# Loading the first batch's v in pieces of 120 and 8 partitions behind a one-partition transfer

## The chip, the core and the metric

The kernel runs on one core of a Trainium2 chip. The metric is the device time of one execution in microseconds (us); less is better. Before the change the median of three runs is 319.89 us (319.6 to 319.95).

## What is computed

Attention with keys and values projected along the sequence (eight batches, eight heads, 1024 positions, head size 64, 64 projected positions), then a layer in which two products of the same input compete and the larger one passes on. All inputs and outputs are float32.

```python
k_proj = einsum('ks,bhsd->bhkd', E, k);  v_proj = einsum('ks,bhsd->bhkd', F, v)
scores = q @ k_proj^T / sqrt(64)
attn   = exp(scores - max) / sum(exp(scores - max))
x      = (attn @ v_proj) laid out as 8192 tokens x 512
out    = maximum(x @ w1, x @ w2) @ w_out          # 512 -> 1024 -> 512
```

## The kernel before

Everything is computed in 16 bits from inputs that are converted as they are loaded. q, k and v of a batch each lie in one tile of 128 partitions (`k_sb`, `q_sb`, `v_sb`): partition p holds positions 8p to 8p + 7 of every head. `load` (line 107) issues such a transfer, or that of some heads only, from GpSimd (POOL in the profile), which also does all the conversions' transfers. The order of all work on all engines is the order of the program's text, written out by hand; a framework adds the semaphores. It also keeps a limited set of semaphores for the transfers that GpSimd issues, so that a transfer can wait in GpSimd's queue until an earlier one has landed.

At the start SyncE loads E, F and the first two heads of k. GpSimd then loads for batch 0: k of heads 2 and 3, q of heads 0 to 3, k and q of heads 4 to 7 (lines 116 to 118), then v in four loads of two heads each:

```python
    for h in range(0, H, 2):
        load(tiles[0], "v", v, 0, h, h + 2)          # lines 122, 123
```

Behind them stand fourteen pieces of the weights w1 and w2 (lines 128 to 142; four at line 130, ten at line 139), the output weights `wo_sb` (line 143), and the loads of batch 1 (line 108, and line 1019 for q). GpSimd issues them one after another.

Batch 0's own steps are written out from line 959 on. `step_eft` turns E and F, `step_kv` (line 183; its matmuls are at line 195, its copies at 205 and 207) projects k or v, `step_qt` turns q (311, 316), `step_sc` forms scores (340) and their exponentials (380), `step_dn` the sums over them (352, 388), `step_inv` the reciprocals (427), `step_at` the products with v (352, 443). `warm` (153) are matmuls on a constant. The order around v is

```python
    step_sc(t, 1, 0)
    step_kv(t, 0, 2, "v"); step_kv(t, 2, 4, "v")
    step_dn(t, 1, 0); step_sc(t, 1, 1); step_at(t, 0, 0); step_at(t, 0, 1); step_inv(t, 1, 0)
    step_kv(t, 4, 8, "v", True, copy=nc.scalar.copy, between=lambda: step_dn(t, 1, 1))
```

(lines 984 to 992, joined here). So the projection of v takes the first two loads one after the other, later the third, and then, behind another sum, the fourth.

Then comes the layer. maximum(a, b) is computed as b + relu(a - b): `wd_sb` = w1 - w2 is formed by VectorE (DVE, lines 541 and 549) as the pieces of weights land, TensorE multiplies x by it (line 525), and turns w2 (557) for a small product w2 x w_out (634). From unit 1 on both large products use a scheme of seven block products with sums of blocks (lines 746 and 838); `T_sb` holds four sums of blocks of `wo_sb` and of that small product, and is written by VectorE at line 597. It is declared at line 580.

Of the kernel before, what the change touches and what calls it, by code (L numbers as in the profile page):

```python
# [10 lines left out]
FP16 = mybir.dt.float16  # L11
# [8 lines left out]
def kernel(  # L20
# [12 lines left out]
    nc = tc.nc  # L33
# [3 lines left out]
    DM = moe_w1.shape[0]  # L37
    DF = moe_w1.shape[1]
    NC = S // 128
# [11 lines left out]
    const = ctx.enter_context(tc.tile_pool(name="const", bufs=1))  # L51
# [13 lines left out]
    def mm_bank(dtype=FP32, n=None):  # L65
        if n is None:
            n = turn.pop(0)
            turn.append(n)
        return ps.tile([128, 512 if dtype == FP32 else 1024], dtype, tag=f"mm{n}", name="mm_ps")
# [37 lines left out]
    def load(t, n, src, b, h0, h1):  # L107
        nc.gpsimd.dma_start(
            out=t[n][:, h0:h1],
            in_=src[b, h0:h1].rearrange("h (p c) d -> p h c d", c=NC),  # L110
        )

    tiles = {b: {} for b in range(B)}
    for n in ("k", "q", "v"):
        alloc(tiles[0], n)
    for h0 in (0, H // 2):
        for n, src in (("k", k), ("q", q)):
            load(tiles[0], n, src, 0, h0 + 2 * ((h0, n) == (0, "k")), h0 + H // 2)
            if (h0, n) == (0, "k"):
                ident = const.tile([128, 128], FP32)  # L120
                make_identity(nc, ident)
    for h in range(0, H, 2):
        load(tiles[0], "v", v, 0, h, h + 2)

    w1_sb = big(1).rearrange("p (r f) -> p r f", r=NDC)
    w2_sb = big(2).rearrange("p (r f) -> p r f", r=NDC)
# [1 line left out]
    for g in range(2):  # L128
        for w_sb, w in ((w2_sb, moe_w2), (w1_sb, moe_w1)):
            nc.gpsimd.dma_start(  # L130
                out=w_sb.rearrange("p (g z) f -> p g z f", z=2)[:, g, :, 0:256],
                in_=w.rearrange("(g p z) f -> p g z f", p=128, z=2)[:, g, :, 0:256],
            )
    for w_sb, w, f0, f1 in (
        (w2_sb, moe_w2, 256, 512), (w1_sb, moe_w1, 256, 512), (w2_sb, moe_w2, 512, DF),
        (w1_sb, moe_w1, 512, 768), (w1_sb, moe_w1, 768, DF),
    ):
        for z in range(2):
            nc.gpsimd.dma_start(
                out=w_sb.rearrange("p (g z) f -> p g z f", z=2)[:, :, z, f0:f1],  # L140
                in_=w.rearrange("(g p z) f -> p g z f", p=128, z=2)[:, :, z, f0:f1],
            )
    nc.gpsimd.dma_start(out=wo_sb, in_=moe_w_out.rearrange("(r p) f -> p r f", p=128))

    ones16 = const.tile([128, 512], FP16)
# [427 lines left out]
    NG = NFB // 2  # L573
    NX = NDC // 2
    CH = DM // 2
# [1 line left out]
    last = len(units) - 1  # L577
    U = {(b, o): {"n": n, "b": b, "o": o, "t": tiles[b]} for n, (b, o) in enumerate(units)}

    T_sb = const.tile([128, 4, NG + NX, CH], FP16)  # L580


    box = {}
# [536 lines left out]
    for b in range(3, B):  # L1120
        t = tiles[b]
        n = 2 * b - 3
# [13 lines left out]
    for i, (new, old) in enumerate(zip([*groups[1:], none], groups)):  # L1136
        n, h = divmod(i + 2, 2)
# [54 lines left out]
    for reg in regs:  # L1192
# [4 lines left out]
        out=mm_bank()[0:1, 0:1], lhsT=ones16[:, 0:1], rhs=ones16[:, 0:1], start=True, stop=True  # L1197
# [166 lines left out]
```

## Time and profile before

| | us |
|---|---|
| median of 3 runs | 319.89 |
| profiled execution, its own time | 320.29 |
| its span, first to last instruction | 318.5 |
| TensorE (PE) busy | 311.8 |
| VectorE (DVE) busy | 241.1 |
| ScalarE (ACT) busy | 206.0 |
| GpSimd (POOL) busy | 41.4 |

Times in the profile are microseconds from the span's start. PE is TensorE's matmuls, PEld its weight loads, which overlap them. A row of a timeline has the start, the length, the engine and line, the operation, what it writes and reads, and a count; a bracket at its end says how long the engine had been idle and what it waited for. A wait for several things is put down to the one that came last. In rows of transfers the size is that of the destination, in 16 bits.

### The profile page before, as it was taken

To read this page: it belongs to the slowest core of one execution; us is meant where nothing else is said; L and a number is where in the kernel's file an instruction comes from. 1 tells how busy PE (TensorE), PEld (TensorE's weight loads), DVE (VectorE), ACT (ScalarE), POOL (GpSimd) and SP (SyncE) were. 2 spreads that over 40 slices of the span, in tenths; PEclk is the share of its full clock that TensorE was granted. 3 is DMA by queue.
4 is the path that set the end of the run, shared out by engine and by line. 5 is a ranking of instruction groups with operands and counts; after the bars stand their busy time and mean duration, and the time that the engine had idled before them with its cause. 6 is when DMAs were issued, how large, how long until landed. Compare 5 with 4: busy or idle time off the path is not lost.

```text
span 318.5 us, 9309 instructions
## 1 busy us (share of the span) xinstructions
PE 311.8 (98%) x3922; PEld 253.8 (80%) x3922; DVE 241.1 (76%) x442; ACT 206.0 (65%) x373; POOL 41.4 (13%) x63
## 2 busy tenths in 40 slices
PE   7999999999999999999999999999999999999996
PEld 3565588888887888788887888788887888888885
DVE  2366889887969696896969696996969696969883
ACT  2386742777776777477776777477776777765541
POOL 8259102004000300012000400030000000000000
PEclk9999999999999999999999999999999999999999
DMA  7999999999989999799999999989979131313124
GB/s 179 206 202 197 207 207 201 207 156 141 204 163 183 171 209 245 208 188 147 225 229 219 169 199 245 221 155 174 230 153 217 42 101 36 102 35 102 36 99 136
DMA packets 76684, 53.71 MB, mean 169 GB/s; under 512 B 29664, under 2 KB 76128, under 8 KB 76640
## 3 DMA queue, kind: packets, MB, share of 16 engines
q0 software_dynamic: 30688, 28.05, 56.0%
q1 hardware_dynamic: 45664, 24.85, 33.1%
q8 instruction: 31, 0.51, 0.6%
q10 hardware_dynamic: 288, 0.20, 0.2%
q14 instruction: 13, 0.11, 0.1%
HBM read 57.15 MB, written 16.78 MB: 232 GB/s over the span
## 4 chain that ended last, share of the span: by engine, by line
PE 95%; DMA 3%; ACT 1%; DVE 1%; issue 0%; POOLq 0%
PE mm_ps L838 47%; PE mm_ps L746 27%; PE mm_ps L525 4%; PE mm_ps L195 4%; PE att_ps L352 4%; PE mm_ps L340 2%; DMA k_sb<-in_k_dram 2%; PE mm_ps L634 2%; PE att_ps L237 1%; PE mm_ps L311 1%; PE mm_ps L153 1%; DMA out_dram<-o_sb 1%; PE att_ps L340 0%; DVE qt_sb L316 0%; ACT ld_sb L388 0%
## 5 line engine op out<-in xcount | busy, mean ns | idle before, releaser
L720 ACT COPY p_sb<-mm_ps 128x512 f32<-128x512 f32 x179 | 101.7, 592 | 49.2 <-PE mm_ps L746 27.3
L838 PEld LDWEIGHTS <-big 128*128 128x128 f16 x768 | 73.5, 98 | 11.8 <-issue 3.6
L838 PE MATMUL mm_ps<-T_sb,big 128*128 128x256 f16 x576 | 76.9, 273 | 0.0
L761 DVE TENSOR_TENSOR gt_sb<-mm_ps,p_sb 128x512 f16<-128x512 f32 x56 | 38.5, 688 | 43.0 <-PE mm_ps L746 41.6
L746 PE MATMUL mm_ps<-big,big 128*128 128x256 f16 x336 | 50.4, 273 | 0.0
L746 PEld LDWEIGHTS <-big 128*128 128x128 f16 x448 | 43.8, 98 | 5.1
L838 PE MATMUL mm_ps<-wo_sb,gt_sb 128*128 128x256 f16 x256 | 42.6, 273 | 0.0
L838 PEld LDWEIGHTS <-gt_sb 128*128 128x128 f16 x376 | 35.7, 98 | 6.7 <-issue 2.7
L469 ACT ACTIVATE ex_sb<-mm_ps 128x512 f16<-128x512 f32 x50 | 27.2, 597 | 18.0 <-PE mm_ps L340 12.3
L746 PEld LDWEIGHTS <-wd_sb 128*128 128x128 f16 x336 | 32.9, 98 | 3.8
L746 PE MATMUL mm_ps<-xt_sb,wd_sb 128*128 128x256 f16 x224 | 32.8, 273 | 0.0
L499 DVE TENSOR_TENSOR xt_sb<-att_ps,ld_sb 128x1024 f16<-128x1024 f32 x26 | 31.7, 1219 | 0.2
L303 POOL COPY junk<-qt_sb 1x1 f16<-1x1 f16 x6 | 2.6, 432 | 172.3 <-DMA qt_sb<-q_sb 172.3
L838 PE MATMUL mm_ps<-m_sb,xt_sb 128*128 128x256 f16 x128 | 24.4, 273 | 0.0
L869 DVE TENSOR_TENSOR o_sb<-mm_ps,p_sb 128x512 f32<-128x512 f32 x32 | 21.9, 683 | 2.8 <-ACT p_sb L898 2.0
L764 DVE TENSOR_SCALAR gt_sb<-gt_sb 128x512 f16<-128x512 f16 (+1 forms) x60 | 20.9, 348 | 2.1
L706 DVE TENSOR_TENSOR big<-gt_sb 128x1024 f16<-128x1024 f16 x32 | 21.9, 683 | 0.0
L838 PE MATMUL mm_ps<-wo_sb,big 128*128 128x256 f16 x128 | 21.5, 273 | 0.0
L807 ACT ACTIVATE gt_sb<-mm_ps 128x512 f16<-128x512 f32 x28 | 16.8, 601 | 5.7 <-PE mm_ps L746 5.7
L838 PE MATMUL mm_ps<-T_sb,gt_sb 128*128 128x256 f16 x120 | 20.3, 273 | 0.0
L838 PEld LDWEIGHTS <-xt_sb 128*128 128x128 f16 x188 | 18.3, 98 | 2.3 <-issue 0.2
L761 DVE TENSOR_TENSOR gt_sb<-p_sb 128x512 f16<-128x512 f32 x28 | 19.1, 682 | 0.6 <-ACT p_sb L720 0.6
(121 smaller groups left out, 434.8 us busy)
## 6 DMA issues: line engine op xcount, KB each, us to landing
out_dram<-o_sb SPq DMA_DIRECT2D x62, 256.0 KB
k_sb<-in_k_dram POOLq DMA_DIRECT2D x7, 1024.0 KB, 9.7
v_sb<-in_v_dram POOLq DMA_DIRECT2D x7, 1024.0 KB, 15.4
q_sb<-in_q_dram POOLq DMA_DIRECT2D x5, 1024.0 KB, 22.8
q_sb<-in_q_dram POOLq DMA_DIRECT2D x6, 512.0 KB, 15.9
big<-in_moe_w_dram POOLq DMA_DIRECT2D x12, 128.0 KB, 6.4
v_sb<-in_v_dram POOLq DMA_DIRECT2D x4, 256.0 KB, 14.0
wo_sb<-in_moe_w_out_dram POOLq DMA_DIRECT2D x1, 1024.0 KB, 10.4
```

The costliest lines, as they stand in the source:

```text
L195: nc.tensor.matmul(out=kv_ps[r * KP : (r + 1) * KP, h * D : (h + nh) * D], lhsT=eft[i][:, c, :], rhs=t[w][:, h0 + h : h0 + h + nh, c, :], ...
L352: nc.tensor.matmul(out=dst(r ^ (hh % 2))[hh * Z : (hh + 1) * Z, :], lhsT=weights(rows, hh), rhs=ex[rows, hh % 2, hh // 2 * W : (hh // 2 + ...
L469: nc.scalar.activation(out=t["ex", g, j][:, e, :], in_=banks[e], func=ACTF.Exp, scale=scale)
L499: nc.vector.tensor_tensor(out=x_out(t, g, j).rearrange("q z o n -> q o z n"), in0=at_ps.rearrange("q o (z n) -> q o z n", z=2), in1=ld[:, ...
L706: nc.vector.tensor_tensor(out=S(i), in0=S(0) if x is None else x, in1=y(), op=op)
L720: copy(out=x, in_=bank)
L746: nc.tensor.matmul(out=bank[:, m * W : (m + 1) * W], lhsT=w_[:, n_, (2 * d + m) * 128 : (2 * d + m + 1) * 128], rhs=a[:, n_, :], start=(n ...
L761: nc.vector.tensor_tensor(out=c_blk(j, c), in0=two(x), in1=two(y), op=ALU.add)
L764: nc.vector.tensor_scalar_max(ap, ap, 0.0)
L807: nc.scalar.activation(out=out, in_=in_, func=ACTF.Relu)
L838: nc.tensor.matmul(out=bank[i][:, 0:CH] if two_banks else bank[:, i * CH : (i + 1) * CH], lhsT=a(c)[:, i * 128 : (i + 1) * 128], rhs=w_(c) ...
L869: nc.vector.tensor_tensor(out=o_sb, in0=two(x), in1=two(y), op=ALU.add)
```

## The change

Batch 0's four v loads each become two transfers, one of partitions 0 to 119 and one of partitions 120 to 127. A transfer of one partition with 16 elements of E goes ahead of them, and another of three partitions ahead of `wo_sb`; both write a corner of `T_sb` that is overwritten later. For this `T_sb` is declared earlier, with the same size.

```diff
+    T_sb = const.tile([128, 4, (DF + DM) // 256, DM // 2], FP16)
+
+    def turn_engines(n):
+        nc.gpsimd.dma_start(out=T_sb[0:n, 3, 0, 0:16], in_=E[0:n, 0:16])
+
+    def load_parts(out, in_, n=120):
+        for p in slice(0, n), slice(n, 128):
+            nc.gpsimd.dma_start(out=out[p], in_=in_[p])
+
+    turn_engines(1)
     for h in range(0, H, 2):
-        load(tiles[0], "v", v, 0, h, h + 2)
+        if h in (0, 2, 4, 6):
+            load_parts(
+                tiles[0]["v"][:, h : h + 2], v[0, h : h + 2].rearrange("h (p c) d -> p h c d", c=NC)
+            )
+        else:
+            load(tiles[0], "v", v, 0, h, h + 2)
...
+    turn_engines(3)
     nc.gpsimd.dma_start(out=wo_sb, in_=moe_w_out.rearrange("(r p) f -> p r f", p=128))
...
-    T_sb = const.tile([128, 4, NG + NX, CH], FP16)
```

## The prediction

> **What bounds the kernel now.** I read the page first, for the engine that fills the span and for the chain that ended last.
>
> ```profile
> span 318.5 us, 9309 instructions
> PE 311.8 (98%) x3922; PEld 253.8 (80%) x3922; DVE 241.1 (76%) x442; ACT 206.0 (65%) x373; POOL 41.4 (13%) x63
> PE 95%; DMA 3%; ACT 1%; DVE 1%; issue 0%; POOLq 0%
> ```
>
> The first row is the span, the second each engine's busy time, the third the chain's shares. TensorE is busy for 311.8 of 318.5 us, so 6.7 us of the span are not matmuls, and only a part of those can have to do with batch 0's v. The v loads matter around 18 to 24 us, so I next read the chain of waits there (start, length, what), then the timeline of the same stretch.
>
> ```profile
> 18.50 0.34 PE att_ps L340 x16
> 18.84 1.20 PE mm_ps L195 x32
> 20.04 0.29 PE att_ps L352 x8
> ...
> 20.36 0.60 ACT ld_sb L388
> 20.95 0.91 ACT ex_sb L380
> 21.87 0.52 ACT ld_sb L427
> 22.38 0.50 ACT ld_sb L388
> 22.89 0.33 ACT vp_sb L207
> ...
> 23.25 0.63 PE att_ps L352 x32
> 23.89 1.83 PE mm_ps L525 x8
> ```
>
> Line 195 multiplies by v. The chain passes through its first 32 matmuls (heads 0 to 3, two loads of two heads) and then stays with ScalarE for almost three microseconds, until the up projection at line 525 begins; behind that TensorE has work without a break. So a gain or a loss of this change must come out of the stretch from 18.8 to 23.9 us, or of weights that come late behind it.
>
> ```profile
> 18.91 1.02 ACT L380 ACTIVATE ex_sb<-att_ps 128x1024 f16<-128x1024 f32 x1 [0.57 <-PE att_ps L340]
> 19.40 0.48 PEld L195 LDWEIGHTS <-eft 128*64 128x64 f16 x16 [0.15 <-DMA v_sb<-in_v_dram]
> 19.98 0.30 PE L352 MATMUL att_ps<-ex_sb,ones 64*32 64x256 f16 x8
> 22.15 0.64 PE L195 MATMUL att_ps<-v_sb,eft 128*64 128x128 f16 x16
> 23.37 0.48 DVE L541 TENSOR_TENSOR wd_sb<-big,big 128x256 f16<-128x256 f16 x2
> 27.22 0.42 DVE L549 TENSOR_TENSOR wd_sb<-big,big 128x512 f16<-128x512 f16 x1 [0.25 <-DMA big<-in_moe_w_dram]
> 27.31 4.48 PE L525 MATMUL mm_ps<-xt_sb,wd_sb 128*128 128x512 f16 x20
> ```
>
> Each row is start, length, engine, line, shape and count; the bracket is the idle time ahead and what ended it. The one wait for v is that of the second load (heads 2 and 3): 0.15 us ahead of 19.40. Why that load is late shows on the GpSimd queue, which issues all these transfers.
>
> ```profile
> 4.86 2.84 POOL L108 DMA_DIRECT2D v_sb<-in_v_dram  x4
> 8.72 0.70 POOL L130 DMA_DIRECT2D big<-in_moe_w_dram  x1 [1.03 <-DMA k_sb<-in_k_dram]
> ...
> 15.98 0.71 POOL L130 DMA_DIRECT2D big<-in_moe_w_dram  x1 [1.84 <-DMA q_sb<-in_q_dram]
> 17.33 0.70 POOL L139 DMA_DIRECT2D big<-in_moe_w_dram  x1 [0.64 <-DMA v_sb<-in_v_dram]
> 19.64 0.71 POOL L139 DMA_DIRECT2D big<-in_moe_w_dram  x1 [1.61 <-DMA v_sb<-in_v_dram]
> 20.65 0.70 POOL L139 DMA_DIRECT2D big<-in_moe_w_dram  x1 [0.30 <-DMA v_sb<-in_v_dram]
> 21.98 5.05 POOL L139 DMA_DIRECT2D big<-in_moe_w_dram  x7 [0.63 <-DMA v_sb<-in_v_dram]
> 27.03 0.88 POOL L143 DMA_DIRECT2D wo_sb<-in_moe_w_out_dram  x1
> ```
>
> Eight transfers go out freely (k, q, k, q, then four of v). The ninth, the first weight, waits for the landing of the first, the twelfth for the fourth, the thirteenth to the sixteenth for the four of v. So a transfer waits for the one eight places ahead of it, and these rows also clock the landings of v: at the latest 17.33, 19.64, 20.65 and 21.98. The steps are 2.31, 1.01 and 1.33 us: the second load is late by about a microsecond, and the rest follow it.
>
> ```profile
> 16.00:18.00 2.00, 2.00 (x36) 1.51 (x36) 0.64 (x2) 1.58 (x4) 1.36 (x2) 1.00 1.24 207
> 20.00:22.00 2.00, 1.72 (x82) 1.32 (x80) 1.32 (x3) 1.65 (x3) 1.07 (x3) 1.00 1.40 195
> 22.00:24.00 2.00, 1.53 (x57) 0.97 (x57) 2.00 (x6) 1.73 (x4) 2.00 (x3) 1.00 1.47 202
> q8 instruction: 1, 0.02, 5.9%
> ```
>
> The first three rows are stretches of 2 us (PE, PEld, DVE, ACT and POOL busy, clock, DMA share, GB/s). The DMA engines are full at about 200 GB/s all through, so what is queued lands in its order, whenever it was issued. The last row is the instruction queue between 17 and 18 us: one packet took 5.9% of 16 engines for 1 us, which is 0.94 us of one engine. That is the late microsecond: whichever engine fetched these instructions works on its share of the second load 0.94 us later, and a load is done when its last engine is.
>
> **The change part by part.** Six transfers are added ahead of the weights and of wo: the one-partition turn, four of 8 partitions, and the three-partition turn. The bytes of v stay the same.
>
> *The v loads.* 128 partitions take 1.33 us (20.65 to 21.98), 8 partitions to an engine if they are spread evenly over 16, so one partition costs 0.166 us. An engine that gets 8 partitions of the 120 and one of the 8 does 9: 0.166 us later per load. An engine that is left out of a 120 gains 1.33 us and can take the 0.94 us fetch without being last. The trace doesn't name engines, so the second load's landing is bounded by 0.94 us earlier (left out) and two extra partitions, 0.33 us, later (not left out). What an earlier landing is worth: the wait is 0.15 us, but line 352 at 19.98 also needs the exponential that ScalarE ends at 18.91 + 1.02 = 19.93. So at most 0.05 us is won; the exponential is what is late next. A later landing costs its whole length. The ends are -0.05 and +0.33 us; I take 0, nearest to the row of the exponential, because the split frees one engine in each of the first two loads.
>
> The Trainium skill, page "DMA: Bandwidth & Descriptors", section "Why a DMA increments its semaphore by 16 and not by 1", says that a transfer from GpSimd runs on the largest number of engines up to 16 that divides its partitions, on consecutive engines from a moving cursor: 15, 8, 1 and 3 here. By that rule a different engine stands out of each of the four 120s, 96 shares come back to the start of the cycle, and the term is anything from -0.05 to +0.33 with the engine of the fetch; no view shows that engine, so the rule leaves my value standing.
>
> *The later v loads.* The fourth is needed at 22.15 and is there by 21.98: 0.17 us of cover. If one engine took an extra partition in every load it would be 4 x 0.166 = 0.66 us late, 0.49 over its cover. If the late engine is freed it lands up to 0.9 us early, which nobody waits for: between is the ScalarE work of the chain. I take 0.
>
> *The added waits.* Each group of line 195 now waits for two landings instead of one. Queued behind that wait on TensorE are lines 352 and 340 and the whole chain. Bounds: 0, and 0.15 us each as for the one wait that is seen; only the second load's lies on the path. I take 0.05 us.
>
> *The GpSimd queue.* The order is now turn, eight v pieces, fourteen weight pieces, turn, wo. Counted with the rule of eight, the second load's 8-partition piece waits for the first k (8.72), the third load's pieces for q and k, the fourth's 120 for the last q, at 15.98. From there GpSimd issues without a real stop at 0.71 us each: the fourth load's two pieces and eight weight pieces begin at 15.98 + 9 x 0.71 = 22.4 with the eighth weight piece, which now begins at 21.98: 0.4 us later. Its landing decides at 27.22.
>
> ```profile
> big<-in_moe_w_dram POOLq DMA_DIRECT2D x1, 128.0 KB, 5.1
> wo_sb<-in_moe_w_out_dram POOLq DMA_DIRECT2D x1, 1024.0 KB, 10.4
> L634 PE MATMUL mm_ps<-wo_sb,big x16: 272/272/273, 39.4 to 41.1; 128*128 128x256 f16 x16
> ```
>
> The first row is that piece: it lands 5.1 us after 21.98, at 27.1. DVE then subtracts until 27.64, and TensorE takes the result behind four matmuls of line 525: 27.31 + 4 x 4.48 / 20 = 28.21. That is 0.57 us of cover, more than the 0.4. And the full DMA engines say that the landing will hardly move, since the piece stood in the queue for most of its 5.1 us. The first weights, issued at 8.72 before and at about 17.4 after, stand behind v in either case. wo is issued later by 0.4 and two turns' worth of issue at most, 1.8 us; it now lands at 27.03 + 10.4 = 37.4 and TensorE first takes it at 39.4, a cover of 2.0. The turns write a corner of T_sb, which DVE writes later from wo, so it waits for the second turn too, which is ahead of wo. Value: 0, with 0 to 0.3 us as bounds.
>
> Sum: 0 + 0 + 0.05 + 0 = +0.05 us. The profiled execution took 320.29 us for its span of 318.5; the 1.8 us around it don't change. It is 0.40 us above the median of 319.89, and I add the sum to that: 319.94, told as **319.95 us**. About 0.2%, 0.64 us, is what a measurement of this kernel can tell from no change.
>
> **The rivals.** *The fetch is not dodged.* The fetching engine is none of those left out early, and carries extra partitions: the second load 0.17 to 0.33 us later, the fourth up to 0.49 over its cover. The chain moves by about 0.3 us: 320.2. For it: only one engine of sixteen can be left out at a time. That the 120 are spread over all sixteen anyway, so that the change does nothing, comes to the same or less.
>
> *Slower: the issue on GpSimd becomes the bound.* From 15.98 the weights hang on GpSimd's pace. An issue of the new shapes, 120 and 8 partitions, is in no row; the rows of whole tiles say 0.70 to 0.88. If it costs c, the eighth weight piece begins 0.4 + 2(c - 0.71) later; from c = 0.8 the 0.57 us of cover is gone. At twice 0.71, c = 1.42, it is 1.8 late, less 0.57: 1.3 us on the path, 321.2. Against it: the 5.1 us is mostly queueing, so a late issue needn't be a late landing. Beside it, the Trainium skill's page "DMA: Bandwidth & Descriptors", section "Rules for kernel authors", advises one transfer of 128 partitions over two of parts, and transfers of 1 MiB and more; this change goes the other way, and the rows of v, with 1.33 us for a load behind another, show no fixed cost that the stream doesn't hide.
>
> *Faster: the stretch closes up.* If all v and weights land up to 0.9 us sooner and ScalarE's chain is paced by them after all, TensorE's idle time between 20 and 24 us could go: (2.00 - 1.72) + (2.00 - 1.53) = 0.75 us, 319.15. Against it: the chain from 20.36 to 23.2 is ScalarE's own work, and the DVE at 23.37 follows its own queue.
>
> **How the numbers follow.** Forecast 0.50 (319.8 to 320.1); fetch not dodged 0.18; GpSimd-bound 0.20; faster 0.12. The first two lie within 0.2% but for 0.02 of the second: same 0.66, slower 0.22, faster 0.12. The range takes the first two, 0.68, and reaches on to 319.3 and to 321.0, into the nearer parts of the two others. The likeliest case's own range is 319.8 to 320.1.
>
> **What would show it.** Right: the wait at 19.40 gone or no longer than now, the exponential at the same place, the steps of v's landings even, TensorE's idle time from 20 to 24 us still about 0.75 us, the eighth weight piece issued at about 22.4 and its DVE row within 0.5 us of 27.22. Wrong: GpSimd rows of the new transfers over 0.8 us, line 525 waiting for DVE behind 27 us, a wait for v at line 195 of over 0.5 us, or the up projection beginning more than 0.6 us off 23.89.

## The result: 1.8 us slower

The changed kernel takes 321.69 us in the median of 14 runs, the kernel before 319.90 in 14 runs beside it: a ratio of 1.0056 [1.0043, 1.007]. The forecast was 319.95, its range 319.3 to 321.0. The runs of the change reach from 320.4 to 322.8 us, most of those before from 319.5 to 320.1.

The 1.8 us have two parts. In every one of the 14 runs the time exceeds its span by 2.08 to 2.18 us, where the kernel before has 1.80 in the median: 0.32 us lie outside the span. The other 1.5 us are in it (median span 319.6, before 318.1; the 318.1 and the 1.80 are medians of the runs of the kernel before beside the experiments). The profiled execution took 322.34 us.

The page's span, busy times and shares of the chain, and then the chain of waits of the changed kernel (start, length, what):

```profile
span 320.2 us, 9319 instructions
PE 312.2 (97%) x3922; PEld 253.7 (79%) x3922; DVE 242.1 (76%) x442; ACT 206.2 (64%) x373; POOL 43.7 (14%) x69
PE 88%; DMA 7%; POOL 4%; issue 0%; DVE 0%; POOLq 0%
```

```profile
5.38 12.82 DMA v_sb<-in_v_dram
18.21 0.28 issue
18.49 2.84 POOL big L145 x4
21.33 4.87 POOL big L154 x7
26.20 7.80 DMA big<-in_moe_w_dram
...
34.02 0.44 DVE wd_sb L565
...
34.50 6.80 PE mm_ps L541 x30
41.30 6.11 PE mm_ps L649 x56
```

TensorE's work is the same, 312.2 us against 311.8. The chain, which before ran through TensorE and ScalarE from v on, now runs through the first v transfer, eleven issues on GpSimd, and the landing of a weight piece at 34.0 us. Lines behind the change are shifted by 14 to 16 (195 is now 211, 525 is 541, 541 is 557, 549 is 565, 130 is 145, 139 is 154).

The timeline of TensorE and VectorE in the changed kernel (start, length, engine, line, shape, count; in brackets the idle time ahead and its end):

```profile
18.68 0.64 PE L211 MATMUL mm_ps<-v_sb,eft 128*64 128x128 f16 x16 [0.77 <-DMA v_sb<-in_v_dram]
19.81 0.64 PE L211 MATMUL mm_ps<-v_sb,eft 128*64 128x128 f16 x16 [0.49 <-DMA v_sb<-in_v_dram]
22.55 0.64 PE L211 MATMUL att_ps<-v_sb,eft 128*64 128x128 f16 x16
24.93 1.90 PE L541 MATMUL mm_ps<-xt_sb,wd_sb 128*128 128x512 f16 x8 [0.65 <-DVE wd_sb L557]
28.43 4.48 PE L541 MATMUL mm_ps<-xt_sb,wd_sb 128*128 128x512 f16 x20
32.82 0.42 DVE L565 TENSOR_TENSOR wd_sb<-big,big 128x512 f16<-128x512 f16 x1 [0.92 <-DMA big<-in_moe_w_dram]
34.02 0.42 DVE L565 TENSOR_TENSOR wd_sb<-big,big 128x512 f16<-128x512 f16 x1 [0.77 <-DMA big<-in_moe_w_dram]
```

Two rows of the same view of the kernel before show the start of the up projection and the subtraction of the pieces that are late at 32.8 and 34.0 in the changed one:

```profile
23.82 1.90 PE L525 MATMUL mm_ps<-xt_sb,wd_sb 128*128 128x512 f16 x8
30.71 0.84 DVE L549 TENSOR_TENSOR wd_sb<-big,big 128x512 f16<-128x512 f16 x2
```

TensorE waits 0.77 and 0.49 us for v, 0.65 us for the first weights, and VectorE waits again for weights at 32.8 and 34.0. The delay can be followed from row to row. The projection of the fourth load begins at 22.55 instead of 22.15, 0.40 us late: that is v's part. The up projection begins at 24.93 instead of 23.82, 1.11 late, because of the wait for the first weights. The twenty matmuls at 28.43 are 1.12 late, no more. The small product begins at 41.30 instead of 39.59 in the chain, 1.71 late, because of the pieces at 32.8 and 34.0. So v carries 0.40 and the weights 1.31 of the 1.7 us that this execution's span is longer. GpSimd's queue in the changed kernel:

```profile
4.86 0.55 POOL L125 DMA_DIRECT2D T_sb<-in_E_dram  x1
5.38 2.09 POOL L129 DMA_DIRECT2D v_sb<-in_v_dram  x3
7.67 0.55 POOL L129 DMA_DIRECT2D v_sb<-in_v_dram  x1 [0.20 <-issue]
10.61 0.75 POOL L129 DMA_DIRECT2D v_sb<-in_v_dram  x1 [2.39 <-DMA q_sb<-in_q_dram]
13.11 0.54 POOL L129 DMA_DIRECT2D v_sb<-in_v_dram  x1 [1.75 <-DMA k_sb<-in_k_dram]
15.66 1.29 POOL L129 DMA_DIRECT2D v_sb<-in_v_dram  x2 [2.01 <-DMA q_sb<-in_q_dram]
18.49 2.84 POOL L145 DMA_DIRECT2D big<-in_moe_w_dram  x4 [1.54 <-DMA v_sb<-in_v_dram]
21.32 7.06 POOL L154 DMA_DIRECT2D big<-in_moe_w_dram  x10
```

A piece of 8 partitions costs GpSimd 0.54 us, one of 120 0.75, the transfer of one partition 0.55. The places in which k and q had let four weight pieces go out between 8.72 and 15.98 are now taken by pieces of v. The first weight goes out at 18.49. The ten issues from 21.32 on take 7.06 us, 0.706 each, so the eighth piece goes out at 21.32 + 3 x 0.706 = 23.44, where it went at 21.98.

Two stretches, 16 to 22 and 22 to 30 us (PE, PEld, DVE, ACT, POOL busy, clock, DMA share, GB/s), first of the kernel before, then of the changed one:

```profile
16.00:22.00 6.00, 5.72 (x165) 3.96 (x164) 3.19 (x7) 4.59 (x8) 2.81 (x5) 1.00 1.29 202
22.00:30.00 8.00, 7.53 (x97) 4.21 (x97) 5.39 (x12) 5.53 (x11) 7.55 (x10) 1.00 1.37 197
```

```profile
16.00:22.00 6.00, 4.74 (x140) 3.30 (x138) 2.49 (x6) 3.68 (x6) 4.46 (x7) 1.00 1.21 182
22.00:30.00 8.00, 6.61 (x94) 3.76 (x93) 5.85 (x13) 4.81 (x9) 7.85 (x12) 1.00 1.21 155
```

The DMA engines no longer move about 200 GB/s all through, but 182 and then 155. From 16 to 30 us that is 0.12 + 0.34 = 0.46 MB less, about 2.3 us of transfers at 200 GB/s.

### The profile page after: what moved, and what is told of

Same layout as the page of the kernel before. It is cut to its first block, busy times and chain, and to the rows that moved or that the text cites. A ratio compares the mean times of both kernels' runs of the same rounds, so it can differ in the third digit from the quotient of the medians.

```text
span 320.2 us, 9319 instructions
## 1 busy us (share of the span) xinstructions
PE 312.2 (97%) x3922; PEld 253.7 (79%) x3922; DVE 242.1 (76%) x442; ACT 206.2 (64%) x373; POOL 43.7 (14%) x69
## 4 chain that ended last, share of the span: by engine, by line
PE 88%; DMA 7%; POOL 4%; issue 0%; DVE 0%; POOLq 0%
PE mm_ps L853 46%; PE mm_ps L761 27%; DMA v_sb<-in_v_dram 4%; PE att_ps L368 3%; PE mm_ps L211 3%; PE mm_ps L356 2%; DMA big<-in_moe_w_dram 2%; PE mm_ps L541 2%; PE mm_ps L649 2%; POOL big L154 2%; PE att_ps L253 1%; POOL big L145 1%; DMA out_dram<-o_sb 1%; PE mm_ps L327 1%; POOL k_sb L108 0%; POOL q_sb L108 0%
## 5 line engine op out<-in xcount | busy, mean ns | idle before, releaser
L853 PEld LDWEIGHTS <-big 128*128 128x128 f16 x768 | 73.5, 98 | 11.8 <-issue 3.6
L761 PE MATMUL mm_ps<-xt_sb,wd_sb 128*128 128x256 f16 x224 | 32.8, 273 | 0.0
L779 DVE TENSOR_SCALAR gt_sb<-gt_sb 128x512 f16<-128x512 f16 (+1 forms) x60 | 21.9, 365 | 2.1
```

The costliest lines, as they stand in the source:

```text
L761: nc.tensor.matmul(out=bank[:, m * W : (m + 1) * W], lhsT=w_[:, n_, (2 * d + m) * 128 : (2 * d + m + 1) * 128], rhs=a[:, n_, :], start=(n ...
L779: nc.vector.tensor_scalar_max(ap, ap, 0.0)
L853: nc.tensor.matmul(out=bank[i][:, 0:CH] if two_banks else bank[:, i * CH : (i + 1) * CH], lhsT=a(c)[:, i * 128 : (i + 1) * 128], rhs=w_(c) ...
```

## The experiments

The theory to be tested: it is the number of transfers ahead of the weights that costs, each taking a place in GpSimd's queue and 0.5 us or more of its issue, whatever it carries; the weights then go out too late, and the DMA engines run short of queued work. The rivals are that the uneven pieces of 120 and 8 partitions burden single engines, that the wait for v is what costs, and that the issue is dear for the new shapes.

**Even halves**, and **the two small transfers alone**. The first changes the size of the pieces, the second leaves v whole.

```diff
-    def load_parts(out, in_, n=120):
+    def load_parts(out, in_, n=64):          # e1_halves
...
-        if h in (0, 2, 4, 6):
+        if h in ():                          # e2_turns
```

> The changed kernel with pieces of 64 and 64 partitions instead of 120 and 8: the same number of transfers in the same order, but each piece is a multiple of 16 partitions. Theory A (the doubled number of transfers makes the weights wait for the landing of v's first piece, and the transfers' engines run short of work): as slow as the changed kernel, 321 to 322 us, GB/s between 20 and 32 us at 130 to 190, the first weight issued at about 17.3 to 18.5. Theory B (the uneven pieces land late because one engine gets more than its share): back to 319.8 to 320.2 us, and GB/s near 200.

> Only the two small transfers of one and three partitions; v in four whole loads as before. Theory A: 319.8 to 320.2 us, because the first weight then waits for the first q (about 10.6) and the transfers' engines stay full. Theory B: the same. A third one, that the small transfers themselves hold something up: 320.5 or more.

Halves: 321.57 us, 1.0053 [1.004, 1.0065], the same loss. The two small transfers alone: 319.95, 1.0003 [0.9995, 1.0012], nothing. So the loss doesn't need the uneven shape. (It may have a share in v's lateness: in the profiles TensorE waits 0.42 us for v with halves and 1.26 with 120 and 8.) The Trainium skill, page "DMA: Bandwidth & Descriptors", section "Rules for kernel authors", advises one transfer of 128 partitions over two halves, because both halves use the same engines. The outcome agrees (1.0053); that the price comes from the number of transfers is seen in the next two runs and not in that sentence.

**Tiny transfers in the same places, v whole.**

```diff
+    def tiny(i):
+        nc.gpsimd.dma_start(out=T_sb[0:16, 3, 0, 16 * i : 16 * i + 16], in_=E[0:16, 0:16])
...
+    tiny(0)
     for h in range(0, H, 2):
         load(tiles[0], "v", v, 0, h, h + 2)
+        tiny(1 + h // 2)
...
+    tiny(5)                                   # ahead of wo_sb
```

> v in four whole loads as before, and six tiny transfers of 16 partitions in the places where the change has its added ones (one ahead of v, one behind each v load, one ahead of wo): the count of transfers alone, with v's shape untouched. Theory A: slow, 320.7 to 321.7 us, with GB/s under 190 between 20 and 32 us. Theory B: 319.8 to 320.2 us.

321.47 us, 1.0055 [1.0042, 1.0067]. Five transfers of half a kilobyte each ahead of the weights cost what the change costs, and TensorE's matmuls don't wait for v there at all; only its weight loads do, for 0.3 us, where it was 0.15. The number alone is enough for a loss of this size.

**Fewer of them, and none ahead of the weights.** A split of the second load alone (with the one-partition transfer, two are added ahead of the weights), three tiny ones, and six tiny ones behind `wo_sb`:

```diff
-        if h in (0, 2, 4, 6):
+        if h in (2,):                         # e5_one_split
...
+        if h < 4:
+            tiny(1 + h // 2)                  # e9_three_tiny, with tiny(0)
...
     nc.gpsimd.dma_start(out=wo_sb, in_=moe_w_out.rearrange("(r p) f -> p r f", p=128))
+    for i in range(6):                        # e10_behind
+        tiny(i)
```

> Only the second v load (heads 2 and 3) split into 120 and 8 partitions, behind the one-partition transfer; the other three whole (an eight-partition small transfer ahead of wo): the change's own uneven pieces, but two transfers more ahead of the weights instead of five. If the count ahead of the weights sets the loss: 319.8 to 320.4 us, the first weight waits for the second k (about 12.8), the eighth is issued by about 22. If uneven pieces cost by themselves: over 320.5, with a wait for v at the second half of v's first projections.

> v whole, three tiny transfers of 16 partitions: ahead of v, behind its first and behind its second load. Three more ahead of the weights instead of five. If the count sets the loss, it is in between: 319.9 to 320.8 us, the eighth weight piece issued between 21.7 and 22.5 instead of about 23. If the tiny transfers cost by themselves: three fifths of e3's loss, about 320.8.

> v whole, and the six tiny transfers of 16 partitions all behind wo, so none ahead of the weights. If their place ahead of the weights is what costs: 319.8 to 320.2 us, GB/s near 200 up to 30 us. If six more transfers on the queue cost wherever they stand: 320.8 or more.

One split: 320.28, 1.0008 [0.9999, 1.0017]. Three tiny: 319.95, 0.9989 [0.9967, 1.0012]. Six behind: 320.33, 1.0013 [0.9992, 1.0035]. All three intervals hold 1. TensorE does wait for v in each, 0.7, 0.4 and 0.4 us, and at most 0.4 us of median span comes of it. And with six behind, the up projection begins at 23.60 and the small product at 39.31 us, no later than in the chain of the kernel before (23.89 and 39.59; the change has 41.30). These two rows of its chain:

```profile
23.60 1.83 PE mm_ps L541 x8
...
39.31 6.11 PE mm_ps L649 x56
```

**Between.** Three of the four loads split (three added), all four split without the small transfers (four), and four tiny ones:

```diff
+        if h in (0, 2, 4):                    # e13_three_splits, no turn_engines
...
+        if h in (0, 2, 4, 6):                 # e14_no_turns, no turn_engines
...
+        if h < 6:
+            tiny(1 + h // 2)                  # e15_four_tiny, with tiny(0)
```

> The change without its two small transfers and with the fourth v load whole: three loads split into 120 and 8, three transfers more ahead of the weights. If the count ahead of the weights sets the loss, as with three tiny transfers: 319.8 to 320.6 us, the eighth weight piece issued by about 22.4 and GB/s over 185 from 20 to 30 us. If the uneven pieces cost: three quarters of the change's loss, 321.0 to 321.4.

> The change without its two small transfers: all four v loads split, four transfers more ahead of the weights. Count: between three and five, 320.2 to 321.4 us, the eighth weight piece issued between 22.4 and 23.4. If only the cursor of the engines that the small transfers move matters: either back at 319.9 or as slow as the change, 321.6.

> v whole, four tiny transfers of 16 partitions: ahead of v and behind its first three loads. Count: the same as the four splits without small transfers, 320.2 to 321.4 us. If shape matters too: faster than those by over 0.3 us.

1.003 [1.0012, 1.0047], 1.0051 [1.0034, 1.0069] and 1.0023 [1.0001, 1.0045]. With tiny transfers the loss sets in between three and four. Splits lose earlier and more, which the theory of a bare number doesn't say: the four splits are about 0.7 us slower than the four tiny ones, over the 0.3 us that the expectation had set for "shape matters too", though the intervals overlap. Three splits came out in the time that the count had given (320.56 us), but the engines moved 162 GB/s from 22 to 30 us where over 185 was expected. In the profiles splits make TensorE wait longer for v: 1.3 us with three splits and 0.4 with three tiny ones, 1.2 and 0.6 with four. With three splits:

```profile
20.18 0.64 PE L209 MATMUL mm_ps<-v_sb,eft 128*64 128x128 f16 x16 [0.65 <-DMA v_sb<-in_v_dram]
24.58 1.90 PE L539 MATMUL mm_ps<-xt_sb,wd_sb 128*128 128x512 f16 x8
```

The up projection is 0.76 us later than in the kernel before, the small product no more than that, and TensorE's matmuls wait for no weight. The span is 0.9 us longer than that of the profiled execution before, so v's lateness is nearly the whole loss there.

**Other orders of the same number.** All five tiny ones ahead of v, all five between v and the weights, and the change's own pieces with the four small ones first:

```diff
+    for i in range(5):
+        tiny(i)                               # e16_tiny_ahead: ahead of v
...
+    for i in range(5):
+        tiny(i)                               # e17_tiny_behind_v: behind v
...
+    for p in slice(120, 128), slice(0, 120):  # e18_small_first
+        for h in range(0, H, 2):
+            nc.gpsimd.dma_start(out=tiles[0]["v"][p, h : h + 2], in_=...[p])
```

> v whole, five tiny transfers of 16 partitions all ahead of v, one ahead of wo: the same count ahead of the weights as in the change, but the first four weight pieces now wait for tiny transfers (done at about 16) and only the next four for v's loads. If the waits for v's landings cause the loss: 319.8 to 320.4 us, the fourth weight piece issued by about 19 and the eighth by about 22, GB/s over 185 from 20 to 30 us. If the count alone: 321.5.

> v whole, the five tiny transfers all behind v and ahead of the weights: the first three weight pieces wait for v's second, third and fourth load (about 19, 20.4 and 21.7). If the waits for v's landings cause the loss: worse than the change, 322.5 to 325 us, with the first product of x waiting for w1 - w2 for 2 us or more. If the count alone: 321.5.

> The change's own transfers in another order: behind the one-partition transfer the four pieces of 8 partitions, then the four of 120. The first four weight pieces then wait for the pieces of 8 and the eighth-place waits for the 120s come behind them. Waits for v's landings as the cause: 319.8 to 320.6 us. Uneven pieces as the cause: 321 to 322 as the change. Count alone: 321.5.

1.0068 [1.0043, 1.0093], 1.0122 [1.0106, 1.0138] and 1.0086 [1.0052, 1.0119]. A variant of the theory, that the weights suffer only where they wait for late landings of v, fell with the first and the third: there small transfers hold the places and the weights don't wait for v, and the loss is no smaller. The second came out where that variant had put it (323.87 us, in 322.5 to 325): where weights do wait for late landings of v, it costs more. Ahead of v the last three loads of v themselves go out late. GpSimd's timeline with all ahead of v, and then with all behind v:

```profile
13.22 0.71 POOL L108 DMA_DIRECT2D v_sb<-in_v_dram  x1 [1.75 <-DMA k_sb<-in_k_dram]
15.79 1.41 POOL L108 DMA_DIRECT2D v_sb<-in_v_dram  x2 [1.85 <-DMA q_sb<-in_q_dram]
17.18 2.79 POOL L146 DMA_DIRECT2D big<-in_moe_w_dram  x4
```

```profile
16.94 0.48 POOL L125 DMA_DIRECT2D T_sb<-in_E_dram  x1 [0.86 <-DMA v_sb<-in_v_dram]
19.22 0.75 POOL L146 DMA_DIRECT2D big<-in_moe_w_dram  x1 [1.79 <-DMA v_sb<-in_v_dram]
```

Behind v each tiny transfer waits for a landing of k, q or v before it takes its own place, and the first weight goes out at 19.22, the latest of all.

**Fewer, larger weight pieces**, to give places back: the last four pieces of w1 merged into two, in the changed kernel and, as a control, in the kernel before. And a coarser split: the loads of heads 0 to 3 as one of 120 and 8 partitions.

```diff
-        (w1_sb, moe_w1, 512, 768), (w1_sb, moe_w1, 768, DF),
+        (w1_sb, moe_w1, 512, DF),             # e11_fewer_weights, e12_before_fewer
...
+    load_parts(tiles[0]["v"][:, 0:4], v[0, 0:4].rearrange("h (p c) d -> p h c d", c=NC))
+    for h in (4, 6):                          # e4_three
+        load(tiles[0], "v", v, 0, h, h + 2)
```

> The changed kernel with the last four pieces of w1 (columns 512 to 1023) as two of twice the size: two issues of GpSimd less behind the first weights. If the pace of GpSimd's issues, 0.71 us each, behind its wait for v holds up the later weights: 0.3 to 1.0 us faster than the change, 320.7 to 321.4, with the waits at line 541 near 34 us smaller. If only the first weights' lateness counts: unchanged, 321.4 to 321.8.

> The kernel before with the last four pieces of w1 as two of twice the size, the control for the same edit in the changed kernel: a piece of twice the size lands later for the first half of its readers, by about 0.7 us. With the 1 us that TensorE has in hand there before: 319.8 to 320.3 us. If the bigger pieces cost wherever they stand: 320.5 to 321.5.

> Heads 0 to 3 of v in one load of 120 and 8 partitions behind the one-partition transfer, heads 4 to 7 in two whole loads as before (an eight-partition small transfer ahead of wo): uneven pieces, but only one transfer more than before ahead of the weights. Theory A: 319.8 to 320.4 us, the first weight issued by 10.9, GB/s near 200. Theory B: 320.5 to 321.5 us, with the wait at the second half of v's first projections.

The merge made the change worse, 1.0095 [1.0065, 1.0126], and cost the kernel before 1.0015 [1.0007, 1.0024]. VectorE takes a piece when all of it is there, and waits longer for the larger one; its row in the changed kernel with the merge:

```profile
33.89 0.43 DVE L565 TENSOR_TENSOR wd_sb<-big,big 128x512 f16<-128x512 f16 x1 [1.95 <-DMA big<-in_moe_w_dram]
```

So the merge doesn't test the places; the changed kernel with it, at 322.83 us, came out above both of its expected ranges. The coarse split gave 1.0049 [1.0036, 1.0062], but TensorE waits 1.7 us for the joint load of four heads, the up projection and the small product are both 1.26 us later than before, and no matmul of TensorE waits for a weight. So this run says nothing on the number either; it shows that a load of v that is late enough costs by itself.

**The queue, put together.** "Begun" is the number of weight pieces that GpSimd has begun to issue by 20.0 us in the profile; "excess" is the median span of the fast runs less that of the kernel before in the same comparison. The columns "begun" and "GB/s" are from one profiled execution, so the last column gives the excess of that execution too.

| kernel | added ahead of the weights | begun by 20 us | GB/s, 22 to 30 us | excess, us | profiled one, us |
|---|---|---|---|---|---|
| before | 0 | 6 | 197 | 0 | 0.4 |
| six behind wo | 0 | 6 | 195 | 0.1 | 0.4 |
| small transfers alone | 1 | 6 | 200 | 0.2 | 0.0 |
| one split | 2 | 5 | 197 | 0.4 | 0.5 |
| three tiny | 3 | 4 | 191 | 0.1 | 0.2 |
| four tiny | 4 | 4 | 172 | 1.0 | 1.0 |
| three splits | 3 | 3 | 162 | 0.5 | 1.2 |
| five tiny | 5 | 3 | 165 | 1.35 | 1.0 |
| even halves | 5 | 3 | 164 | 1.5 | 0.8 |
| the change | 5 | 3 | 155 | 1.5 | 2.1 |
| four splits | 4 | 3 | 146 | 1.7 | 1.5 |
| small pieces first | 5 | 3 | 184 | 2.0 | 1.8 |
| all tiny behind v | 5 | 1 | 138 | 3.6 | 3.3 |

(All tiny ahead of v has 5 begun, 1.55 us and 1.8 in the profiled execution, and 170 GB/s already from 16 to 22 us, where the last loads of v go out late; with small pieces first it was 159 there.) Two further readings show how far a shortage of queued work explains the lower rate. One is the DMA queue of GpSimd from 23 to 24 us (packets, MB, share of 16 engines), before and after the change:

```profile
q0 software_dynamic: 397, 0.19, 142.8%
```

```profile
q0 software_dynamic: 241, 0.12, 98.5%
```

The other is the same row from the start to 22 us, before, after, and with three tiny transfers:

```profile
q0 software_dynamic: 3615, 3.21, 90.8%
```

```profile
q0 software_dynamic: 3674, 3.13, 89.6%
```

```profile
q0 software_dynamic: 3681, 3.20, 91.3%
```

By then GpSimd has issued k, q and v, 22 heads of 0.131 MB or 2.88 MB, and its finished pieces of weights, 0.131 MB each: seven before (3.80 MB), four after (3.41), six with three tiny (3.67). Issued but not yet moved are thus 0.59, 0.28 and 0.47 MB. With 0.47 the engines keep 191 GB/s, with 0.28 they don't. And GpSimd, at 0.706 us for 0.131 MB, adds at most 0.186 MB/us until the eighth piece is out, less than the 0.2 the engines can take.

That a small reserve is the cause of the low rate is not shown, though. The same row of the changed kernel up to 27 us and from 27 to 29, and of all tiny ahead of v up to 21 us and from 21 to 23:

```profile
q0 software_dynamic: 5227, 3.88, 95.6%
q0 software_dynamic: 328, 0.26, 110.9%
```

```profile
q0 software_dynamic: 3128, 2.89, 86.5%
q0 software_dynamic: 516, 0.26, 113.9%
```

By 27 us twelve pieces are issued in the changed kernel, two of them of twice the size, or 4.72 MB with k, q and v: 0.84 MB are issued and not moved, more than in the kernel before at 22 us, and yet the engines move 0.13 MB/us. With all tiny ahead it is five pieces by 21 us, a reserve of 0.65 MB, and again 0.13 MB/us. So a small reserve goes with the low rate around 22 to 24 us, but something else must keep the rate low later. What that is no view shows. What the rows do show is that the first weights are issued later, that weights land later, and that they are waited for.

**Outside the span.** Every kernel with six more GpSimd instructions than before shows 2.07 to 2.12 us outside the span in the median, six transfers behind `wo_sb` included (2.12, so that its 1.0013 is all there), and every one with up to four 1.77 to 1.82. Five and twelve tiny transfers behind `wo_sb`, and six small memsets on GpSimd in their place, were to tell what it hangs on.

```diff
+    for i in range(5):                        # e19_five_behind; 12: e20_twelve_behind
+        tiny(i)
...
+    for i in range(6):                        # e21_six_memsets
+        nc.gpsimd.memset(T_sb[0:16, 3, 0, 16 * i : 16 * i + 16], 0.0)
```

> Five transfers of 16 partitions by 16 elements behind the output weights instead of six. Asked is the time outside the span (the execution's time less its span), 1.8 us for the kernel before and every kernel with up to four added transfers, 2.1 us for every kernel with six. If it is a step in the number of instructions or transfers of GpSimd, it is 1.8 or 2.1 here, with nothing between. If it goes by the number, 2.05. The span itself within 0.2 us of the one before (318.1) in both, since the weights are ahead of the transfers.

> Twelve such transfers behind the output weights. Time outside the span: 2.1 us if it is one step between four and six; about 2.4 if it grows with the number (0.32 for six). The span may be up to 0.5 us longer than before from batch 1's loads, which are issued 6 us later.

> Six small memsets on GpSimd in the place of the six transfers behind the output weights: as many GpSimd instructions, no added transfer. Time outside the span: 1.8 us if the 0.32 belongs to transfers, 2.1 if it belongs to GpSimd's instructions. The span within 0.2 us of the one before.

Outside the span: 1.89 us with five, 1.81 with twelve, 2.11 with six memsets (medians of 8, 2 and 8 runs). So the 0.32 us don't belong to transfers, and are neither a step nor a slope in their number; they came with six more GpSimd instructions, and with twelve, in two runs, they were gone again. What lies in that time no view shows. The ratios are 0.9994 [0.9973, 1.0015], 1.02 [1.0108, 1.0292] and 0.9991 [0.9964, 1.0019].

With twelve the span missed its expectation: 327.06 us, 7.05 us more span, where at most half a microsecond was expected. GpSimd's timeline there, TensorE's behind it, and a stretch of 2 us (the clock is the figure before the last two):

```profile
32.18 0.96 POOL L125 DMA_DIRECT2D T_sb<-in_E_dram  x2 [0.87 <-DMA big<-in_moe_w_dram]
37.30 2.39 POOL L125 DMA_DIRECT2D T_sb<-in_E_dram  x5 [4.17 <-DMA wo_sb<-in_moe_w_out_dram]
39.68 0.93 POOL L108 DMA_DIRECT2D k_sb<-in_k_dram  x1
```

```profile
49.65 1.06 PE L253 MATMUL att_ps<-k_sb,eft 128*64 128x256 f16 x16 [1.16 <-DMA k_sb<-in_k_dram]
54.47 1.92 PE L253 MATMUL att_ps<-v_sb,eft 128*64 128x256 f16 x16 [3.75 <-DMA v_sb<-in_v_dram]
```

```profile
56.00:58.00 2.00, 2.00 (x13) 1.19 (x10) 1.00 (x4) 0.67 (x3) 1.32 (x2) 0.50 1.45 199
```

The eight places are full of tiny transfers and `wo_sb`; the next waits for `wo_sb` to land, and batch 1's k goes out at 39.68 instead of 27.91. TensorE then waits 1.16 and 3.75 us for batch 1's loads. That is 4.9 of the 7.05 us. The clock explains most of the rest: it was granted at 0.50 from 52 to 58 us, where the kernel before has 1.00, and the sixteen matmuls at 54.47 take 1.92 us instead of 1.04, the twelve behind them 2.48 instead of 1.48. The places are taken as in the change, at another spot and with a larger loss.

## Why the prediction was wrong

**The GpSimd queue** is the term that failed: 0 with bounds of 0 to 0.3, where the span grew by 1.5 us. In the profiled execution the weights carry 1.31 us of it. The term was wrong in three of its steps.

"From there GpSimd issues without a real stop": it stood 1.54 us ahead of 18.49 for the landing of v, so that the eighth weight piece went out at 23.44 and not at 22.4. The prediction's own rule of eight says so: the first weight, now fourteenth in the queue, waits for the sixth transfer, which is the first piece of v. The count was broken off at the fourth load of v.

"The landing will hardly move": the two pieces issued from 23 to 24 us, the eighth among them, took 4.9 us to land, where it was 5.1. So that landing moved by about 1.2 us, nearly as much as the issue, 1.46. This piece was not what TensorE waited for in the end, since TensorE was itself 1.1 us late when it came to it.

"The first weights ... stand behind v in either case": they were what TensorE waited for, 0.65 us ahead of 24.93. Before, four of them had been issued by 15.98; now the first goes out at 18.49. The rest, 0.60 us, came from the eleventh and twelfth piece, which the prediction didn't look at. The premise that the engines are "full at about 200 GB/s all through" held for the old order only: they went from 197 to 155 GB/s.

**The second load of v**, 0 with bounds of -0.05 and +0.33, came out at 0.40, just outside its bounds: TensorE waited 0.77 us for the first load and 0.49 for the second, and 0.40 of this is left at the projection of the fourth. The instruction fetch of 0.94 us of an engine shows from 16 to 17 us in the changed kernel, so it fell into the first load; no view shows that a left-out engine dodged it. That v is not the main cause here is shown by the five tiny transfers, which lost 1.35 us of span without such a wait of a matmul. It is not negligible either: three splits (0.76 us) and the coarse split (1.26 us) lost most of their time by it.

**The later loads of v**: the projection of the fourth, at 22.55 instead of 22.15, had no wait of its own. **The added waits** of 0.05 us are not seen as such; the small transfers alone gave 1.0003. **wo**: VectorE takes it at 40.20 instead of 37.57, in the changed kernel's timeline with a wait:

```profile
40.20 0.69 DVE L612 TENSOR_TENSOR T_sb<-wo_sb 128x1024 f16<-128x1024 f16 x1 [1.16 <-DMA wo_sb<-in_moe_w_out_dram]
```

The row is 2.63 us later, the chain at that place 1.71 (41.30 instead of 39.59 for the small product), and `wo_sb` isn't in the chain: its cover got smaller and held.

**"The 1.8 us around it don't change"** was wrong by 0.32 us, a fifth of the loss.

**The rivals.** "The issue on GpSimd becomes the bound" (0.20, 321.2) named the place and nearly the size. Its condition was wrong: it asked for pieces at over 0.8 us each, and they cost 0.54 to 0.75. It wasn't the price of an issue that decided but the places taken and the weights that no longer went out early. That its 1.3 us on the path are close to what was measured is luck. "Faster" and "the fetch is not dodged" are out by their size.

**What stays open.** Splits cost a little more than as many tiny transfers (three: 1.003 against 0.9989; four: 1.0051 against 1.0023), with intervals that overlap in the second pair. The longer waits for v go with this; what makes v later with splits is not known. Nor is it known why the engines move less when enough is issued. Which engine takes what is in no view, so whether the moving start of the 120s did anything is not known; the prediction's 96 shares count the one-partition transfer as one, while the kept trace has it as 16 packets of two bytes. That the change's runs spread over 2.4 us would fit an engine that is late in some of them; that is only argued. What fills the 0.32 us outside the span is not known.

## What to carry to other kernels

A small transfer is not small to the queue that issues it: it takes a place until it lands and 0.5 us of issue, and what stands behind it goes out later by both. Before transfers are put ahead of a stream, write down for the old and the new order which landing each piece of the stream waits for and when it goes out, down to the last piece, and not only for the one that was nearest to being late. Don't take a landing as fixed because it "is mostly queueing": here it moved by 1.2 us when the issue moved by 1.46.

## What the runs showed of the hardware

- An issue on GpSimd takes 0.48 to 0.55 us for a transfer of 16 partitions by 16 elements, 0.71 for a weight piece of 128 KB and 0.88 for `wo_sb` of 1 MB: nearly a fixed price.
- At 0.706 us for 128 KB GpSimd feeds at most 186 GB/s, below the 200 GB/s that the engines moved.
- With 0.28 MB issued and not moved at 22 us the engines moved 0.12 MB/us from 23 to 24 us; with 0.47 MB they moved 191 GB/s from 22 to 30. But with 0.84 MB at 27 us (the change) and 0.65 at 21 us (all tiny ahead of v) they moved 0.13 MB/us too, so the bytes issued don't fix the rate.
- Twelve tiny transfers behind a 1 MB load moved the next batch's loads by 11.8 us and cost 7.05 us of span. After TensorE's idle time there the granted clock was 0.50 from 52 to 58 us.
- The time outside the span went from 1.80 to 2.11 us with six more GpSimd instructions of any kind, and was 1.81 with twelve (two runs).
